# Order of the first loads of a two-layer SiLU kernel: everything on SyncE's queue, and one dummy matmul more

## The chip, the cores and the metric

One core of one Trainium2 chip. The metric is the device time of one execution in microseconds (us), taken several times; a separate execution is profiled. Kernels of one comparison ran on the same chip, alternating with the kernel before.

## The reference, cut to what matters

```python
B, S, D, F = 1, 2048, 640, 1728          # all bfloat16
h = silu(einsum("bsd,df->bsf", x, w1))
out = einsum("bsf,fd->bsd", h, w2)
```

The first product sums over D, five slabs of 128 (k = 0 to 4), for 2048 rows in four chunks of 512; the second sums over F.

## The kernel before: the parts that the change touches

TensorE needs x with D on the partitions. For chunk 0, the first slab is loaded as it lies (`xk`) and transposed on TensorE; slabs 1 to 4 come through DMA transposes. Dummy matmuls on a zero tile keep TensorE busy until `xk` has landed. `ahead_of_start` puts an instruction ahead of the program's start barrier.

```python
ld_xk = ahead_of_start(lambda: load(sp, xk[:, :, :], x_v[:, 0:SCH // P, 0:P]), ET.SP)
# ...
ld_a[0] = ahead_of_start(lambda: half(act, 0, 0), ET.Activation)   # slab 0 of w1, columns of tiles 0..3
ld_k[0] = half(act, 0, 1)                                          # slab 0, tiles 4..7
ld_a[1] = half(act, 1, 0)                                          # slab 1, tiles 0..3
ahead_of_start(lambda: first(0), ET.SP)                            # DMA transpose, k = 1 and 2
ld_k[1] = ahead_of_start(lambda: half(sp, 1, 1), ET.SP)
ahead_of_start(lambda: slab(2), ET.SP)
first(1)                                                           # DMA transpose, k = 3 and 4
slab(3)
slab(4)
# ...
wait(pe, p_z)
dummies(9)                             # ps <- z: 128x128 by 128x256
wait(pe, ld_xk, p_ident)
# ...
for h in range(2):                     # two transposes on TensorE, one copy on VectorE, twice
    # ...
# ...
wait(pe, ld_a[0], turned0[0])
k_pass(0, range(FH), 0, HB)            # four matmuls of 256 columns
wait(pe, turned0[1])
k_pass(0, range(FH), HB, SCH)          # four of 256
wait(pe, ld_k[0])
k_pass(0, range(FH, FA))               # four of 512
wait(pe, ld_x[1], ld_a[1])
k_pass(1, range(FH))
wait(pe, ld_k[1])
k_pass(1, range(FH, FA))
barrier_wait_here(ET.PE)
for k in range(2, DT):
    wait(pe, ld_x[k], ld_k[k])
    k_pass(k, range(FA))               # eight of 512
```

## Time and profile before

| | before |
|---|---|
| first three executions | 126.7, 126.93, 127.58 us |
| span of the profiled execution | 125.8 us |
| TensorE busy | 122.8 us of it, 591 matmuls |
| first real matmul starts | 3.88 us |
| matmul rate doubles at about | 9.15 us |

The first row is time on the device; all else is one execution of the profile, with times from its first instruction.

### The profile page before, as it was taken

The numbers are of one execution on the slowest core, as the hardware profiler recorded it, in microseconds if no ns is written. First come the engines' busy times: TensorE is split into PE (matmuls) and PEld (weight loads), VectorE is DVE, ScalarE is ACT, GpSimd is POOL, SyncE is SP. The second block draws the span as 40 slices with busy tenths as digits, with TensorE's granted clock in tenths as the row PEclk, the third lists the DMA queues.
The fourth block names the chain that finished last, engine by engine and source line by source line (L and its number), as shares of the span: only waits on it lengthen the run. The fifth ranks groups of instructions, "written<-read, shape, count | busy, mean of one in ns | idle before, by whom it ended". The sixth has DMA issues, their size and how long they took to land.

```text
span 125.8 us, 1358 instructions
## 1 busy us (share of the span) xinstructions
PE 122.8 (98%) x591; PEld 56.0 (45%) x591; DVE 8.0 (6%) x14; ACT 38.1 (30%) x66; POOL 0.8 (1%) x7
## 2 busy tenths in 40 slices
PE   7999999999999999999999999999999999999994
PEld 4534444444444444444444444444444443444452
DVE  0100000000000000000001020200003211012021
ACT  0400695555555555555550101010003011010100
POOL 2000000000000000000000000000000000000000
DMA  5999789895000000000000000000002767111113
GB/s 154 316 296 260 161 156 127 195 388 219 0 0 0 0 5 0 3 0 0 0 0 0 5 0 0 0 0 0 0 0 47 83 225 286 52 52 52 52 52 104
DMA packets 19557, 10.35 MB, mean 82 GB/s; under 512 B 13536, under 2 KB 19168, under 8 KB 19552
## 3 DMA queue, kind: packets, MB, share of 16 engines
q1 hardware_dynamic: 19120, 9.88, 30.1%
q10 hardware_dynamic: 432, 0.39, 0.9%
q8 instruction: 4, 0.07, 0.2%
q14 instruction: 1, 0.01, 0.0%
HBM read 4.64 MB, written 2.62 MB: 58 GB/s over the span
## 4 chain that ended last, share of the span: by engine, by line
PE 96%; DMA 2%; DVE 0%; ACT 0%; issue 0%
PE ps L218 95%; DMA xk<-in_x_dram 2%; PE ps L193 0%; DVE xT L195 0%; ACT o_sb L293 0%
## 5 line engine op out<-in xcount | busy, mean ns | idle before, releaser
L218 PE MATMUL ps<-xT,w1s 128*128 128x512 bf16 (+2 forms) x284 | 61.1, 388 | 0.3 <-DVE xT L195 0.3
L218 PE MATMUL ps<-w2s,hT 128*128 128x512 bf16 (+2 forms) x221 | 45.4, 367 | 0.0
L218 PEld LDWEIGHTS ps<-xT,w1s 128*128 128x128 bf16 (+1 forms) x284 | 27.7, 102 | 33.5 <-issue 2.7
L222 ACT ACTIVATE hT<-ps 128x512 bf16<-128x512 f32 x52 | 30.0, 608 | 28.5 <-PE ps L218 28.5
L218 PEld LDWEIGHTS ps<-w2s,hT 128*128 128x128 bf16 x221 | 20.9, 98 | 24.4 <-issue 1.1
L293 ACT CAST o_sb<-ps 128x512 bf16<-128x512 f32 (+1 forms) x8 | 4.4, 545 | 42.2 <-PE ps L218 42.2
L291 DVE CAST o_sb<-ps 128x512 bf16<-128x512 f32 (+1 forms) x9 | 6.1, 677 | 98.8 <-PE ps L218 98.8
L218 PE MATMUL ps<-hT,w2s 128*128 128x512 bf16 x52 | 11.4, 379 | 0.0
L218 PEld LDWEIGHTS ps<-hT,w2s 128*128 128x128 bf16 x52 | 5.1, 98 | 6.1
L293 ACT CAST oT<-ps 128x512 bf16<-128x512 f32 x2 | 1.1, 588 | 11.0 <-PE ps L218 11.0
L146 PE MATMUL ps<-z 128*128 128x256 bf16 x9 | 2.1, 418 | 0.4 <-DVE z L140 0.4
L203 ACT ACT_TABLE_LOAD x1 | 1.3, 1283 | 3.3 <-ACTq L409 3.3
L218 PE MATMUL ps<-w2t,hTt 64*128 64x512 bf16 (+2 forms) x17 | 2.2, 366 | 0.0
L291 DVE CAST oT<-ps 128x512 bf16<-128x512 f32 x2 | 1.3, 686 | 13.7 <-PE ps L218 13.7
L146 PEld LDWEIGHTS ps<-z 128*128 128x128 bf16 x9 | 1.2, 142 | 0.8 <-DVE z L140 0.4
L222 ACT ACTIVATE hTt<-ps 128x512 bf16<-128x512 f32 x2 | 1.2, 597 | 1.1 <-PE ps L218 1.1
L218 PEld LDWEIGHTS ps<-w2t,hTt 64*128 64x128 bf16 x17 | 0.7, 94 | 1.4 <-issue 0.8
L193 PE MATMUL ps<-ident,xk 128*128 128x128 bf16 x4 | 0.6, 308 | 0.5 <-DMA xk<-in_x_dram 0.5
L193 PEld LDWEIGHTS ps<-ident,xk 128*128 128x128 bf16 x4 | 0.3, 130 | 1.0 <-DMA xk<-in_x_dram 1.0
L195 DVE COPY xT<-ps 128x256 bf16<-128x256 bf16 x2 | 0.5, 290 | 3.1 <-PE ps L193 3.1
L218 PE MATMUL ps<-hTt,w2t 64*128 64x512 bf16 x4 | 0.6, 381 | 0.0
L218 PEld LDWEIGHTS ps<-hTt,w2t 64*128 64x128 bf16 x4 | 0.1, 94 | 0.4 <-issue 0.4
(9 smaller groups left out, 1.4 us busy)
## 6 DMA issues: line engine op xcount, KB each, us to landing
out_dram<-o_sb SPq DMA_DIRECT2D x15, 160.0 KB, 1.9
w2s<-in_w_dram SPq DMA_DIRECT2D x1, 1120.0 KB, 6.0
w2s<-in_w_dram SPq DMA_DIRECT2D x1, 960.0 KB, 8.2
w1s<-in_w_dram SPq DMA_DIRECT2D x3, 256.0 KB, 4.4
w1s<-in_w_dram SPq DMA_DIRECT2D x1, 480.0 KB, 5.2
w1s<-in_w_dram SPq DMA_DIRECT2D x1, 400.0 KB, 6.0
w1s<-in_w_dram ACTq DMA_DIRECT2D x3, 128.0 KB, 2.6
xT<-in_x_dram SPq DMA_TRANSPOSE x11, 4.2
```

Source lines behind the costliest of these rows:

```text
L146: pe.matmul(ps[:, 3, 0:HB], lhsT=z[:, 0:P], rhs=z[:, :], start=True, stop=True)
L193: ins = pe.transpose(v[:, i * P:(i + 1) * P], xk[:, 2 * h + i, :], ident[:, :])
L195: r = tick(dve.tensor_copy(out=xT[:, 0, h * HB:(h + 1) * HB], in_=v[:, 0:HB]), s_dve)
L203: act.activation(out=warm[:, :], in_=warm[:, :], func=ACT.Silu)
L218: return pe.matmul(o, lhsT=l, rhs=r, start=start, stop=stop, skip_group_check=shared)
L222: r = tick(act.activation(out=out_ap, in_=in_ap, func=ACT.Silu), s_act)
L291: r = tick(dve.tensor_copy(out=out_ap, in_=in_ap), s_dve)
L293: r = tick(act.copy(out=out_ap, in_=in_ap), s_act)
```

## The change

Its intent is visible in the diff: let nothing travel beside `xk`, bring the first slab of w1 right behind it, and fill the gap between TensorE's transposes and its first real matmul.

```diff
-        ld_a[0] = ahead_of_start(lambda: half(act, 0, 0), ET.Activation)
-        ld_k[0] = half(act, 0, 1)
-        ld_a[1] = half(act, 1, 0)
+        ld_a[0] = ahead_of_start(lambda: half(sp, 0, 0), ET.SP)
+        ld_k[0] = ahead_of_start(lambda: half(sp, 0, 1), ET.SP)
         ahead_of_start(lambda: first(0), ET.SP)
-        ld_k[1] = ahead_of_start(lambda: half(sp, 1, 1), ET.SP)
+        ahead_of_start(lambda: slab(1), ET.SP)
         ahead_of_start(lambda: slab(2), ET.SP)
@@
             turned0.append(r)
+        dummies(1)
         barrier_wait_here(ET.DVE)
@@
-        wait(pe, ld_x[1], ld_a[1])
-        k_pass(1, range(FH))
-        wait(pe, ld_k[1])
-        k_pass(1, range(FH, FA))
-        barrier_wait_here(ET.PE)
-        for k in range(2, DT):
+        for k in range(1, DT):
             wait(pe, ld_x[k], ld_k[k])
             k_pass(k, range(FA))
+            if k == 1:
+                barrier_wait_here(ET.PE)
```

## The prediction

> **What bounds the kernel now.** I read the page's chain first, then the chain in order of time, because a change to the first loads can only act ahead of the first real matmul or in gaps of TensorE.
>
> ```profile
> ## 4 chain that ended last, share of the span: by engine, by line
> PE 96%; DMA 2%; DVE 0%; ACT 0%; issue 0%
> ...
> 0.00 2.96 DMA xk<-in_x_dram
> 2.96 0.05 issue
> 3.01 0.41 PE ps L193 x2
> 3.42 0.02 issue
> 3.44 0.30 DVE xT L195
> 3.74 0.14 issue
> 3.88 120.07 PE ps L218 x577
> 123.95 0.02 issue
> 123.97 0.27 ACT o_sb L293
> ```
>
> TensorE is the bound: from 3.88 us to 123.95 us 577 matmuls follow each other and the chain names no wait. So loads after the first tile of x (xk) are hidden today. Ahead of it stand 2.96 us of waiting for xk, then 0.92 us from the first transpose to the first matmul. Only two quantities are open to this change: when that first matmul starts, and how fast the matmuls run at first.
>
> For the second I compared matmul forms in the window 0 to 14 us with those of a later window (9.4 to 9.7 us).
>
> ```profile
> L218 PE MATMUL ps<-xT,w1s 128*128 128x512 bf16 x32 | 8.8, 445 | 0.0
> L146 PE MATMUL ps<-z 128*128 128x256 bf16 x9 | 2.1, 418 | 0.4 <-DVE z L140 0.4
> L218 PE MATMUL ps<-xT,w1s 128*128 128x256 bf16 x8 | 1.9, 415 | 0.3 <-DVE xT L195 0.3
> ...
> L218 PE MATMUL ps<-xT,w1s 128*128 128x512 bf16 x3 | 0.8, 380 | 0.0
> ```
>
> Narrow windows give 634 ns for each 512-column matmul up to about 8.8 us, 540 and 414 between 9 and 9.4 us, and 379 to 380 after that. In the timeline of the weight loads the starts 8.10, 8.52, 8.95 lie 0.43 us apart; then 24 starts fall in 5.13 us, 0.214 us apart. So the rate doubles at about **9.15 us**. From 3.88 to 9.15 us TensorE ran at half rate, which costs (9.15 - 3.88) / 2 = 2.6 us. This is the larger prize. The granted clock column says 1.00 throughout, so it does not show this; spacing and duration do.
>
> Then the DMA queues, in the timeline and in narrow windows (q1 is SyncE's, q10 ScalarE's; q1 is packets, MB, share).
>
> ```profile
> 0.00 0.45 SPq L89 DMA_DIRECT2D xk<-in_x_dram  x1
> 0.12 1.47 ACTq L89 DMA_DIRECT2D w1s<-in_w_dram  x3
> ...
> 0.51 1.33 SPq L122 DMA_TRANSPOSE xT<-in_x_dram  x1
> 1.89 1.04 SPq L89 DMA_DIRECT2D w1s<-in_w_dram  x2
> 3.18 1.23 SPq L122 DMA_TRANSPOSE xT<-in_x_dram  x1
> 4.45 2.10 SPq L89 DMA_DIRECT2D w1s<-in_w_dram  x4
> ...
> q1 hardware_dynamic: 534, 0.13, 38.8%
> q10 hardware_dynamic: 199, 0.19, 36.5%
> ```
>
> The last two lines are the window 1.1 to 2.6 us. xk is 128 x 4 runs of 256 B, 512 packets, so nearly all of q1's 534 are xk. In the same time ScalarE's queue moved 0.19 MB: the halves of the first slab share the engines with xk, though the second half is needed only after 5.5 us.
>
> **What the Trainium skill says.** "DMA: Bandwidth & Descriptors", Issuing engines are not separate DMA queues: all queues run on the same 16 engines, and a second issuer saves only issue time. Queues, rings and completion order, on the same page: each engine alternates between queues packet by packet. The trace agrees: 38.8% and 36.5% side by side. With packets of 256 B against 1 KB, xk gets the smaller part of the bytes.
> "TensorE: Matmul & The Clock Gate", Part 1: the array runs at half rate until a window of about 3.4 us was busy, and the windows run freely, so the flip moves between runs. The doubling at 9.15 us agrees: two windows back is 2.3 us, and the window from 2.3 to 5.7 us holds both of TensorE's gaps. Part 4 says that a transpose does not count as busy in the same way; nothing in this trace tells.
>
> **The change, part by part.**
> 1. *The two halves of slab 0 leave ScalarE for SyncE, behind xk.* Inside xk's data time (1.1 to 2.6 us) the other queue moved 0.19 MB. Windows without xk run at 280 to 390 GB/s, so about 0.5 us of engine time is taken from xk at most; part of the trickle before 1.7 us (5 packets of q1 from 1.4 to 1.5 us) is probably latency and stays. I choose 0.4 us: xk lands at about **2.55 us** instead of 2.96. The dummies are no hindrance: the last starts at 2.08 us and occupies the array for 0.21.
> 2. *Is the first half there in time?* From ScalarE it was issued at 0.12 and landed after 2.6 us, at 2.7. Now it is issued at 0.51 behind xk; 128 KB at 350 GB/s is 0.37 us more data, landing at about 2.95 us. It is needed at 2.55 + 0.92 = 3.47 us. Hidden, with 0.5 us spare. The second half, about 3.4 us, is needed 8 x 0.213 = 1.7 us after that. Hidden.
> 3. *Two more issues ahead of the DMA transpose.* Each plain issue costs SyncE about 0.5 us (0.45, and 1.04 for two). The transpose moves from 0.51 to about 1.5 us and, with its 4.3 us to landing, from 4.8 to about 5.6 us (I grant it 0.2 for a quieter start). Slab 1, now whole and 256 KB, is issued at 2.9 us; like slab 2 today (3.2 us) it lands at about 6.1 us. Today all of k = 1 is in by 5.1 us. It is needed after the k = 0 pass, 8 x 0.213 + 4 x 0.427 = 3.4 us at half rate: 6.9 us. Hidden if TensorE stays slow; if it is fast from 4 us on, the pass ends at 5.4 and about 0.6 us shows.
> 4. *Everything later on SyncE slides by about 1 us.* Slab 3 from 4.45 + 4.4 = 8.9 to 9.8 us, slab 4 to about 10.3 us. Today k = 3 starts at about 11.7 us. Hidden. The barrier moves with SyncE by 0.5 us; ScalarE's table load then ends near 5.2 us, long before its first output at 13.75 us.
> 5. *One dummy behind the transposes.* 0.21 us in the 0.44 us between the last transpose's start (3.01 + 4 x 0.107 = 3.44) and the first matmul (3.88). It costs nothing, as the matmul still waits for VectorE's copy, and closes half of that gap. The other gap, from 2.3 us to xk's arrival, shrinks from 0.7 to 0.3 us by part 1.
> 6. *The clock.* Half-rate time after the first matmul is worth half of itself. Today no window could qualify before about 3 us, so the flip falls between roughly 6.7 and 10.3 us; this alone makes 1.8 us of spread, and the three times spread by 0.88. With the gaps smaller, windows from about 2.5 us on may qualify: start and flip come earlier together, and the flip by some 0.4 to 0.8 us more, worth 0.2 to 0.4 us. If even a window from 0.4 us qualifies, the flip comes between 3.8 and 7.2 us, worth 1 us and more.
>
> Sum: -0.4 (start) and about -0.4 (flip, my mean of the cases) on 126.93: **126.1 us**. After 15 us both kernels do the same work.
>
> **Rivals.**
> *A: nothing arrives earlier.* xk's packets trickle until 1.7 us though the engines are nearly idle, so latency or descriptor making may set its end. Then the start stays at 3.9 us, only the dummy acts, and the time is 126.6 to 127. For it: engine share of 5% in that window; against it: q10's 0.19 MB. About 30%.
> *B: start earlier, same half-rate stretch:* 126.3 to 126.5. About 35%.
> *C: the clock flips much earlier* because TensorE is busy almost without a gap from 0.39 us: 124.9 to 125.7, limited by slab 1 at 6.1 us and slab 3 at 9.8 us, which become the next waits. For it: the dummy can have no other purpose. Against it: two gaps of 0.2 to 0.3 us remain. About 30%.
> *D: a new wait replaces the old:* the first half lands later than 3.5 us, or slab 1 after 6.9 us; 127 to 128. The spare of 0.5 us speaks against it. About 5%.
>
> **Range and chances.** A to C span 124.9 to 127, and the free-running window alone moves a median of three runs by some 0.3 us. I take 125.0 to 127.1. Faster by 2% means under 124.4 us: start and flip would both have to come out at their best, 2.5 us in sum; 5%. Slower by 2% means over 129.4 us, a stall of 2.5 us in a load with 0.5 us or more spare; 2%. Within 2%: 93%.
>
> **What would show it.** xk's time to landing (3.0 us now; 2.5 to 2.6 if part 1 holds); the first matmul on w1s in the chain (3.88 now; near 3.45); the time of the change from 634 to 379 ns, against 9.15 us; a wait of TensorE for w1s or xT in the chain after it (none expected: parts 2 to 4); ScalarE's first output at 13.75 us earlier by the whole gain. The prediction is wrong if xk lands at 2.9 us or later with q10 empty, if the chain shows a DMA wait for w1s, or if the flip comes later than today by more than the start gains.

## The result, and the profile after

The changed kernel took **125.72 us** (median of 6, 125.39 to 126.03), the kernel before 127.47 us (median of 6, 126.7 to 128.23). The ratio is 0.987, 95% interval 0.983 to 0.991: faster by 1.3%, within the 2% band. A ratio here is the mean time of one kernel's fast runs over that of the other's fast runs of the same rounds, so not quite the ratio of the two medians. A second series (`r_after` below) gave 0.993, interval 0.989 to 0.997. Over all series the kernel before took 126.93 us on average (39 executions, 125.89 to 128.23) and the changed kernel 125.74 us (12 executions, 125.39 to 126.03): **1.2 us less, and a much narrower spread.** One of those 39 executions carries the mark "slow" (127.87 us); as there is one core, this mark only says that it lay over 1.5% above the fastest of its series.

The chain of the changed kernel, in order of time (start, length, what; pieces under 0.1 us ahead of the last one left out):

```profile
0.38 2.10 PE ps L146 x9
2.49 0.46 PE ps L192 x4
2.94 0.21 PE ps L146
3.21 119.01 PE ps L218 x577
122.24 0.27 ACT o_sb L290
```

The load of xk is gone from this chain, and its view of the changed kernel (`--tile xk --engine SP`) says:

```profile
DMA to landing us min/median/max: 2.3/2.3/2.3
```

It was 3.0 before. TensorE goes from dummies to transposes to one dummy to the first real matmul at **3.21 us**, 0.67 us earlier than before. That the chain no longer names xk does not mean that it stopped setting the start: xk landed at 2.29 us and the first transpose started at 2.34, and in all fourteen profiles, the one of before too, the first transpose starts 0.05 us after xk has landed. In the profile the dummies merely last a little longer (to 2.49 us) than they occupy the array. The 577 matmuls behind it now take 119.01 us where they took 120.07, though they are the same instructions: 1.06 us come from their rate. The two add up to 1.73 us, and the spans differ by 125.8 - 124.1 = 1.7. ScalarE's first output came at 12.02 us instead of 13.75, 1.73 us earlier: the whole gain is made ahead of it, as predicted.

The forms of the changed kernel's matmuls in the window 0 to 14 us:

```profile
L218 PE MATMUL ps<-xT,w1s 128*128 128x512 bf16 x40 | 9.5, 400 | 0.0
L218 PE MATMUL ps<-xT,w1s 128*128 128x256 bf16 x8 | 1.9, 415 | 0.0
```

The mean of a 512-column matmul fell from 445 to 400 ns, because fewer of them ran slow: in narrow windows they take 634 ns until 6.0 us and 380 ns from 6.6 us on. The rate doubles at about **6.35 us**, against 9.15. Slow time after the first real matmul went from 5.27 to 3.14 us; half of the difference is 1.07 us, which is the 1.06 seen in the chain.

Why xk came earlier shows in the DMA engines between 1.3 and 1.7 us. First the kernel before, then the changed one (q1 is SyncE's queue, q10 ScalarE's; packets, MB, share of 16 engines):

```profile
q1 hardware_dynamic: 56, 0.01, 14.9%
q10 hardware_dynamic: 6, 0.01, 5.9%
```

```profile
q1 hardware_dynamic: 342, 0.09, 95.4%
```

In these 0.4 us the changed kernel moved 342 packets, nearly all of xk, and the kernel before 56. The engines of the kernel before were not busy with something else: their shares add up to 21%.

Behind the start, the changed kernel's loads land later, as meant: slab 1 was issued at 2.89 us and landed after 3.3 us, at 6.2; slab 3 at 9.5. In this execution TensorE waited for none of them.

### The profile page after: what moved, and what is told of

Read it like the earlier page. It is cut to its first block, busy times and chain, and to the rows that moved or that the text cites. A ratio compares the mean times of both kernels' runs of the same rounds, so it can differ in the third digit from the quotient of the medians.

```text
span 124.1 us, 1359 instructions
## 1 busy us (share of the span) xinstructions
PE 121.8 (98%) x592; PEld 55.9 (45%) x592; DVE 8.0 (6%) x14; ACT 38.1 (31%) x66; POOL 0.8 (1%) x7
## 4 chain that ended last, share of the span: by engine, by line
PE 98%; ACT 0%; issue 0%; DVEq 0%
PE ps L218 96%; PE ps L146 2%; PE ps L192 0%; ACT o_sb L290 0%; DVEq L406 0%
## 5 line engine op out<-in xcount | busy, mean ns | idle before, releaser
L218 PE MATMUL ps<-xT,w1s 128*128 128x512 bf16 (+2 forms) x284 | 60.0, 383 | 0.0
```

The costliest lines, as they stand in the source:

```text
L218: return pe.matmul(o, lhsT=l, rhs=r, start=start, stop=stop, skip_group_check=shared)
```

## The experiments

In what follows "the doubling" is the time at which the rate of matmuls doubles, read from their lengths (about 420 to 273 ns for 256 columns, 634 to 379 ns for 512), good to some 0.2 us. A profile is a single execution; times are of six. The diffs of `e3_bystander` and `e8_tiny` leave out the spare tile and the wait for these loads at the end. The theory to be tested: (a) xk is early because ScalarE's queue is empty; (b) the doubling is a matter of its own, delayed by idle TensorE ahead of the first real matmul. Rivals: the DMA transpose behind xk was what slowed it; the doubling simply follows the first real matmul; the dummy does it all.

### What slowed xk: two loads beside it

`e3_bystander`: the changed kernel, and ScalarE loads 2 x 128 KB that nobody reads.

```diff
+        by = [ahead_of_start(lambda: load(act, spare[:, 0, :], w1_v[:, 0, 0:SCH]), ET.Activation)]
+        by.append(load(act, spare[:, 1, :], w1_v[:, 0, SCH:2 * SCH]))
         ld_a[0] = ahead_of_start(lambda: half(sp, 0, 0), ET.SP)
```

> The changed kernel, and beside it ScalarE again issues two loads of 128 KB at the places where the kernel before had its first two, into a spare tile that nobody reads. Theory (ScalarE's loads take xk's share of the engines): xk lands at 2.8 to 3.0 us instead of 2.3, the first matmul starts at 3.7 to 3.9 us or later, and 0.5 to 1.5 us of the gain is lost. Rival (the DMA transpose issued right behind xk made it slow, not ScalarE): xk still lands at 2.3 to 2.4 us, and the time stays within 0.3 us of the changed kernel.

Measured: 126.86 us (126.5 to 127.27), ratio to the kernel before 1.0005 (0.996 to 1.005): the whole gain is lost. xk landed at 3.0 us and the first real matmul started at 3.88 us, exactly as in the kernel before. Its queues from 1.3 to 1.7 us:

```profile
q1 hardware_dynamic: 34, 0.01, 8.9%
q10 hardware_dynamic: 4, 0.00, 6.3%
```

The same drought is back, though the order on SyncE is that of the changed kernel. In addition slab 1 landed so late (issued at 3.15 us, 5.0 us to landing) that TensorE waited 1.0 us for it. So the time of this run is not the price of the late xk alone: in the profile the doubling came at 7.0 us, 2.1 us earlier than in the one of before, and this wait took back what that gave. For (a) the landing counts, and not the time. The landing of xk, here and in the next run:

```profile
DMA to landing us min/median/max: 3.0/3.0/3.0
DMA to landing us min/median/max: 2.3/2.3/2.3
```

`e4_early_turn`: the changed kernel with the DMA transpose back directly behind xk; ScalarE's queue stays empty.

```diff
+        ahead_of_start(lambda: first(0), ET.SP)
         ld_a[0] = ahead_of_start(lambda: half(sp, 0, 0), ET.SP)
         ld_k[0] = ahead_of_start(lambda: half(sp, 0, 1), ET.SP)
-        ahead_of_start(lambda: first(0), ET.SP)
```

> The changed kernel with the first DMA transpose moved back to directly behind xk, ahead of the two halves of slab 0; nothing on ScalarE. Theory (ScalarE's loads were what slowed xk): xk lands at 2.3 us as in the changed kernel, but the first half of slab 0 is issued 1.3 us later and lands at about 4.5 to 5 us, so the first matmul waits for it, with a gap of over 1 us behind the dummy; time 126.7 to 128. Rival (the transpose was what slowed xk): xk lands at 2.8 us or later.

Measured: xk landed at 2.3 us, so the transpose was not what slowed it. The price is the expected one and larger: the first half of slab 0 was issued at 1.88 us and took 4.1 us to land. TensorE's timeline of this run (start, length, ..., count, idle before):

```profile
2.76 0.42 PE L146 MATMUL ps<-z 128*128 128x256 bf16 x1
6.05 10.27 PE L218 MATMUL ps<-xT,w1s 128*128 128x256 bf16 x38 [2.87 <-DMA w1s<-in_w_dram]
```

The median is 128.02 us, ratio 1.009 (1.003 to 1.015). The profiled execution (129.29 us) is marked slow; I use it for the landing of xk and of slab 0, and as one row of the table below.

`e8_tiny`: as `e3_bystander`, but 64 B per partition instead of 1 KB.

```diff
+        by = [ahead_of_start(lambda: load(act, spare[:, 0, 0:32], w1_v[:, 0, 0:32]), ET.Activation)]
+        by.append(load(act, spare[:, 1, 0:32], w1_v[:, 0, SCH:SCH + 32]))
```

> The changed kernel and two loads of ScalarE at the places of the former halves, but of only 64 B per partition (8 KB each instead of 128 KB) into a spare tile. If xk is slowed by the bytes that the other queue moves, it lands at 2.3 to 2.4 us and the time equals the changed kernel's. If it is slowed by the second queue being served at all (descriptors made, queues alternated), it lands at 2.7 to 3.0 us, as beside the loads of 128 KB.

Measured: xk at 2.4 us; 125.87 us (125.68 to 126.29), beside 125.79 for the changed kernel on the same chip. Between 1.3 and 1.7 us, xk moved 261 packets while ScalarE's queue moved 98 small ones. So a second queue as such did no harm here; loads of 1 KB per partition did. Together before, `e3_bystander`, `e4_early_turn` and the changed kernel form a square: xk lands at 3.0 us with ScalarE's 128 KB loads and at 2.3 us without, wherever the transpose stands.

### What moves the doubling

`e1_no_dummy`: the changed kernel without its added dummy.

```diff
-        dummies(1)
         barrier_wait_here(ET.DVE)
```

> The changed kernel without its one dummy behind the transposes. Theory (start and doubling of the rate are separate, and the dummy fills a gap that delays the doubling): xk still lands at 2.3 us and the first matmul on w1s still starts at 3.2 us, but the rate doubles later than the 6.35 us of the changed kernel, at 7 to 9 us, and the time is 0.3 to 1 us longer than the changed kernel's 125.7 us. Rival (the doubling comes a fixed time after the first real matmul or by chance of the window, the dummy does nothing): time within 0.2 us of the changed kernel's.

Measured: 125.96 us (125.7 to 126.2), ratio to the kernel before 0.993 (0.989 to 0.998). Its mean, 125.95 us, is 0.2 us above the changed kernel's 125.74, in the direction of the theory, but not from the same series and so not shown. The expected late doubling was a miss: it fell at about 4.7 us in the profiled execution, earlier than in the first profile of the changed kernel. TensorE's timeline of this run:

```profile
3.20 2.70 PE L217 MATMUL ps<-xT,w1s 128*128 128x256 bf16 x12 [0.26 <-DMA w1s<-in_w_dram]
7.05 4.26 PE L217 MATMUL ps<-xT,w1s 128*128 128x512 bf16 x19 [1.14 <-DMA w1s<-in_w_dram]
```

The twelve matmuls of k = 0 are done early, and then TensorE waits 1.14 us for slab 1. An early doubling does not reach the end of the kernel. This is the first sight of a floor.

`e2_dummy_only`: the kernel before plus the dummy.

```diff
             turned0.append(r)
+        dummies(1)
         barrier_wait_here(ET.DVE)
```

> The kernel before with the one dummy behind the transposes and nothing else. Theory: the first matmul stays at 3.9 us; the large gap ahead of the transposes (2.3 to 3.0 us) stays, so the doubling comes at best 0.5 us earlier: 0 to 0.4 us gained. Rival (the dummy is what counts): the doubling falls 3 us after the first matmul as in the changed kernel, at about 7 us, and about 1 us is gained.

Measured: 126.43 us (126.04 to 127.48), ratio 0.999 (0.993 to 1.004). Alone, the dummy shows no effect; in the profile the doubling was at 9.3 us, as in the kernel before.

`e5_bridge`: the kernel before, with its loads, but twelve dummies, so that TensorE has no gap while it waits for xk, and the one dummy behind.

```diff
-        dummies(9)
+        dummies(12)
@@
+        dummies(1)
         barrier_wait_here(ET.DVE)
```

> The kernel before with twelve dummies instead of nine (they then end at 2.95 us, where xk lands) and the one dummy behind the transposes; the loads as before. Theory (TensorE's gaps ahead of the first matmul delay the doubling, whatever closes them): the first matmul stays at 3.9 us, the doubling falls at 6 to 8 us, about 1 us is gained on the kernel before, with the same start. Rival (the doubling counts from the first matmul on w1s alone): no gain, 0 to 0.2 us.

Measured: ratio 0.992 (0.986 to 0.997), median 126.0 us, single executions from 125.31 to 127.45. In the profile xk landed at 3.2 us, the first real matmul started at 4.08 us, later than in the kernel before, and the doubling came at about 5.1 us: span 124.0 us. So TensorE's gaps alone, with the loads untouched and a later start, are worth 0.8% on average (interval 0.3 to 1.4%). The profiled execution is the fastest of the six. The matmuls of 512 columns between 5.7 and 6.2 us, before and in this run:

```profile
L218 PE MATMUL ps<-xT,w1s 128*128 128x512 bf16 x2 | 1.1, 634 | 0.0
L219 PE MATMUL ps<-xT,w1s 128*128 128x512 bf16 x4 | 1.0, 379 | 0.0
```

The rival that the doubling follows the first real matmul falls. The wide spread shows that closing the gaps makes an early doubling possible, not certain.

`e6_few_dummies`: the changed kernel with three dummies instead of nine at the start; TensorE idles 1.1 us ahead of its transposes.

```diff
-        dummies(9)
+        dummies(3)
```

> The changed kernel with three dummies at the start instead of nine: TensorE then idles from about 1 us to 2.3 us. The loads are those of the changed kernel. Theory (gaps delay the doubling): the first matmul stays at 3.2 us, the doubling comes later than with nine, 0.3 to 0.8 us are lost against the changed kernel. Rival (only the start of the first matmul counts): the same time as the changed kernel within 0.2 us.

Measured: 126.34 us (126.0 to 126.55); doubling at 8.2 us in the profile. `e7_two_behind`, on the same chip, differs from it in the dummies alone, with nine ahead and two behind:

```diff
-        dummies(1)
+        dummies(2)
```

> The changed kernel with two dummies behind the transposes instead of one; the second would end at 3.2 us, just where the first matmul starts. Theory: the last gap closes, start unchanged or at most 0.05 us later, the doubling no later; time equal to the changed kernel's or up to 0.3 us less. If the doubling then falls before 5 us, the wait for slab 1 (landing at 6.2 to 6.9 us) takes back what it gives.

Measured: 125.91 us (125.61 to 126.01), doubling at about 3.8 us in the profile; the mean is 0.45 us below that of `e6_few_dummies`, and only the fastest execution of `e6_few_dummies` (126.0 us) reaches the slowest of `e7_two_behind` (126.01). Some 0.1 us of it is the start (3.33 against 3.24 us); the rest is the doubling. The second dummy brings nothing that can be seen against the changed kernel (125.74 us in other series), and the profile suggests why: after the early doubling TensorE waits 1.54 us for slab 1.

All profiles; the gap is TensorE's idle time between the last dummy ahead and the first transpose, the last column the time from the first real matmul to the doubling:

| profile | gap ahead of the transposes | first real matmul | doubling | after the first matmul |
|---|---|---|---|---|
| before | 0.7 us | 3.88 | 9.15 | 5.3 |
| `e2_dummy_only` | 0.8 | 3.97 | 9.3 | 5.4 |
| `e6_few_dummies` | 1.3 | 3.33 | 8.2 | 4.9 |
| `e4_early_turn` | 0.1, then 2.9 behind | 6.05 | 11.2 | 5.2 |
| `e3_bystander` | 0.7 | 3.88 | 7.0 | 3.1 |
| changed, first profile | 0.1 | 3.21 | 6.35 | 3.1 |
| `e8_tiny` | 0.1 | 3.30 | 6.0 | 2.7 |
| `e9_slab1_act` (below) | 0.1 | 3.29 | 5.5 | 2.2 |
| `e9b_slab1_act` (below) | 0.1 | 3.25 | 5.2 | 2.0 |
| `e10_slab1_first` (below) | 0.1 | 3.27 | 4.8 | 1.5 |
| `e5_bridge` | 0.3 | 4.08 | 5.1 | 1.0 |
| `e1_no_dummy` | 0.1 | 3.20 | 4.7 | 1.5 |
| `e7_two_behind` | 0.1 | 3.24 | 3.8 | 0.6 |
| changed, second profile | 0.2 | 3.30 | 3.6 | 0.3 |

(A gap is counted from the start of the last dummy plus its 0.21 us of spacing; the idle times that the profile prints are about 0.2 us shorter, as it lets a matmul last until its result is out.) With a gap of 0.7 us or more the doubling comes 3.1 to 5.4 us after the first real matmul in these profiles; with a gap of 0.3 us or less, 0.3 to 3.1 us. Within each group it moves from one execution to the next. A row is one execution, and often an extreme one: the fastest of its six in `e5_bridge`, both `e9` runs and the first profile of the changed kernel, the slowest in `e2_dummy_only`, `e3_bystander`, `e4_early_turn`, `e10_slab1_first` and the second profile. The comparison of kernels rests on the times of six, not on this table.

Five traces (`e3_bystander`, `e5_bridge`, `e8_tiny`, `e9_slab1_act`, `e9b_slab1_act`) also hold clock records that no view prints by time. In them the full clock starts at 7.00, 5.19, 6.13, 5.53 and 5.31 us, within 0.13 us of the readings above, and lasts 119.47 us in each, which is 35 times 3.413 us, the length of window that the prediction counts with, though the spans differ by up to 2.2 us. This lets the table be sorted by an estimate, made after the fact from starts and spacings: going back from each doubling in steps of 3.41 us, the step that ends at the doubling holds at most 0.6 us of idle TensorE in every profile. The step before it lies inside the program in the first five rows, and holds 0.96 to 1.6 us there; in the others it begins ahead of the first instruction. So closing the gap matters where it brings the idle time of a step under this mark, which lies somewhere from 0.6 to 0.96 us; where the steps fall changes from one execution to the next.

### The floor, and two ways to lower it

`r_after`: the changed kernel again.

> The changed kernel again, as the measure for the other three of this call on the same chip. Expected 125.4 to 126.1 us in every run, a spread of less than half of that of the kernel before, because an early doubling is stopped by slab 1 (landing at 6.2 to 6.9 us).

Measured: 125.79 us, all six between 125.57 and 125.87, while the kernel before on this chip ranged from 125.89 to 127.87. In the profile the doubling came at 3.6 us, almost at once. TensorE's timeline of this run, and the line of its waits:

```profile
2.43 0.61 PE L192 MATMUL ps<-ident,xk 128*128 128x128 bf16 x4
2.83 0.42 PE L146 MATMUL ps<-z 128*128 128x256 bf16 x1
3.30 2.03 PE L218 MATMUL ps<-xT,w1s 128*128 128x256 bf16 x12
6.90 4.48 PE L218 MATMUL ps<-xT,w1s 128*128 128x512 bf16 x20 [1.56 <-DMA w1s<-in_w_dram]
```

```profile
PE ps L218 <- DMA w1s<-in_w_dram: 1.6, 1, 1.6
```

The first pass ends at 5.33 us, and TensorE waits until slab 1 is there; k = 1 starts at 6.90 us. The span is 124.5 us, *longer* than the 124.1 us of the first profile, where the doubling came 2.7 us later but slab 1 happened to land at 6.2 us. This would explain the narrow spread: a late doubling costs, an early one is cut off by slab 1. `e9b_slab1_act` below puts it to the test.

`e10_slab1_first`: slab 1 issued ahead of the DMA transpose.

```diff
-        ahead_of_start(lambda: first(0), ET.SP)
         ahead_of_start(lambda: slab(1), ET.SP)
+        ahead_of_start(lambda: first(0), ET.SP)
```

> The changed kernel with slab 1 issued ahead of the first DMA transpose instead of behind it; all still on SyncE. Theory (slab 1 behind the 1.3 us issue of the transpose is the floor of the changed kernel's fast runs): xk at 2.3 us, first matmul at 3.2 us, slab 1 issued at 1.5 us and landing at about 4.8 us, the transpose issued at 2.0 us and landing at 5.6 to 6 us; TensorE waits for k = 1 until 6 us at most, and the time is 0.2 to 0.6 us less than the changed kernel's on the same chip, with single runs below 125.2 us. Rival (the transpose lands as late as slab 1 did, or the doubling is rarely early enough): no gain.

Measured, on the chip of `r_after`: 125.5 us (124.95 to 125.88), mean 125.46 against 125.75, so 0.3 us less than the changed kernel; one execution was the first below 125 us. The wait for slab 1 is gone (issued at 1.5 us, landed after 3.2 us, at 4.7; the transpose after 3.7 us, at 5.7). With the doubling at 4.8 us, the profile, which is of the slowest of the six executions, shows the next floor. Its chain:

```profile
5.47 4.77 DMA w1s<-in_w_dram
10.24 0.14 issue
10.37 112.34 PE ps L218 x549
```

Slab 3, issued at 5.47 us, lands at 10.24, and TensorE waited 0.95 us for it.

`e9_slab1_act`: slab 1 in two halves from ScalarE's queue, issued only after xk has landed.

```diff
-        ahead_of_start(lambda: slab(1), ET.SP)
+        wait(act, ld_xk)
+        ld_h10 = half(act, 1, 0)
+        ld_k[1] = half(act, 1, 1)
```

(and a separate wait of TensorE for each half, as in the kernel before).

> The changed kernel with slab 1 loaded in two halves from ScalarE's queue, which first waits for xk to have landed, so that it cannot take anything from xk. Theory (once the doubling comes early, slab 1 is the next wait): xk lands at 2.3 us, the first matmul starts at 3.2 us or up to 0.2 us later, slab 1 lands at 5 to 5.6 us instead of 6.2 to 6.9, no wait for it stays; time 0 to 0.5 us less than the changed kernel's. Rival (it now takes engine time from the second half of slab 0 and the transposes, which become the wait): no gain.

Measured: 125.8 us (125.07 to 126.33), ratio to the kernel before 0.992 (0.987 to 0.996). xk at 2.4 us, doubling at 5.5 us, no wait of TensorE for a load: span 123.7 us, the shortest profile so far. Once more, beside the changed kernel (`e9b_slab1_act`, same kernel):

> Slab 1 in halves from ScalarE's queue behind a wait for xk, once more, beside the changed kernel on the same chip. Theory: no wait for slab 1 in any run, 0 to 0.5 us less than the changed kernel, with a wider spread than it (125.0 to 126.4 us), as nothing stops an early doubling. Rival: equal means, the extra queue costs at the start what it gives later.

Measured: 125.61 us (125.04 to 126.15), mean 125.61 against 125.75 for the changed kernel on the same chip, doubling at 5.2 us, span 123.7 us again. As expected the spread is wider (1.1 us, and 1.3 in the run before, against 0.3 here and 0.6 in the changed kernel's first series), as nothing cuts an early doubling off. The 0.14 us between the means is too little against this spread to be called shown. For `e10_slab1_first` the 0.3 us is about twice the uncertainty of the difference (0.13 us, from the scatter of the six and six executions); I call it likely. The two were not combined.

## Why the prediction was right, point by point

The predicted 126.1 us was 0.8 us below before's time of then; the changed kernel took 125.7 us, inside the range, and 1.2 us less than the kernel before over all series. Both mechanisms were right; both were taken too small. The number itself was a mean over cases, and the case that was given the best chance, B (126.3 to 126.5 us, 35%), did not occur: none of the 12 executions lies there. What the profiles show is C, given 30%.

1. **Part 1, xk earlier: right, but mis-sized.** 0.7 us instead of 0.4. The step that failed reads "part of the trickle before 1.7 us ... is probably latency and stays". It did not stay: 56 packets of xk became 342. I had counted the bytes that ScalarE's queue takes from xk. Some half of the loss lies in 0.4 us in which hardly anything moves on either queue: at the changed kernel's 342 packets in 0.4 us, the 286 that are missing are worth 0.33 us (an estimate). The rest fits the sharing that I had counted (from 1.7 to 2.1 us q10 took 53.6% of the engines, q1 45.0%). The 38.8% and 36.5% "side by side" were means over 1.1 to 2.6 us and hid the still part; nor did packets alternate one for one, with 162 of q1 and 73 of q10 from 1.7 to 2.1 us. Rival A, built on the same reading, falls with it.
2. **Part 2, the first half in time: right, with a smaller spare.** It landed at 0.5 + 2.6 = 3.1 us, not 2.95, and was needed at 3.2, not 3.47. The spare was 0.1 us, not 0.5; in `e6_few_dummies` TensorE even waited for it by about 0.16 us. (The wait that the profile of `e1_no_dummy` puts down to it cost nothing: the first real matmul comes 0.87 us after the first transpose there, as before and after the change.) The next gain at the start would have to move this load as well.
3. **Part 3, slab 1 hidden if TensorE is slow, showing if it is fast: right, but mis-sized.** It landed at 6.2 to 6.9 us, not 6.1, and an early doubling showed 1.1 to 1.6 us of waiting, not 0.6. The prediction contradicted itself here: it allowed for such a wait, and yet it named a DMA wait for w1s in the chain as a sign that it was wrong. The first profile has none, the second has one (DMA 3% of its chain). Nor are landing times of one profile constants: with the loads of before, all of k = 1 was in by 5.0 us in its own profile, but only by 6.6 us in `e2_dummy_only` and 6.0 in `e5_bridge`.
4. **Part 4, the rest hidden: right for the changed kernel.** Slab 3 landed at 9.5 us in the first profile (9.8 was expected). That it would be the wait after slab 1 (rival C) was seen in `e10_slab1_first`. ScalarE's table load ended at 5.6 us, not 5.2, as it moved by 1.0 us and not 0.5; it stayed hidden.
5. **Part 5, the dummy costs nothing: right.** That it helps is not shown: alone it gave 0.999, and taking it away gave 125.95 us against 125.74 in other series, too close to call. What matters is the other gap, ahead of the transposes. Rival C's argument for itself ("the dummy can have no other purpose") was a guess at an intent, not evidence.
6. **Part 6, the clock: right in kind, too small.** I weighted it with 0.4 us; the first profile shows 1.06 us, the second about 0.7 us after the wait for slab 1 (1.3 us of span less 0.6 us of start). Over all series 1.2 us less 0.6 us of start leaves 0.6 us. Both profiles of the changed kernel show case C, with the doubling 2.8 and 5.6 us earlier than in the one of before; C's time, 124.9 to 125.7 us, was met by 5 of the 12 executions; the others lie up to 0.33 us above it. That slab 1, the wait that C named, landed later than it said fits this, but is not tested by itself. The 1.8 us of spread forecast for the kernel before was about right: 1.5 to 2.0 us in its four series. Rival D did not occur.

What stays open: why xk stands nearly still from 1.3 to 1.7 us when ScalarE's loads of 1 KB per partition arrive, though the engines are then mostly idle and small loads on the same queue do not do it. `e8_tiny` made ScalarE's loads smaller and their runs shorter at once, so which of the two matters is open too. And whether the dummy behind the transposes is worth 0.2 us or nothing.

## What to carry to other kernels

In the first microseconds, give the load that everything waits for an empty machine: loads that are needed later belong behind it, also when another queue would issue them "for free" (here two of 128 KB cost 0.7 us, two of 8 KB less than 0.1). Look at the length of matmuls, not at busy time, and keep TensorE without gaps from its first dummy to its first real work; then check what the faster start runs into, since the next load in line sets the floor. When a tuned kernel's time scatters (here by 1.8%, and by 0.5% after the change), the reason for the scatter may be the thing to tune: here it gave about half of the gain.

## What the Trainium skill lacked or had wrong

- "DMA: Bandwidth & Descriptors", Issuing engines are not separate DMA queues: it says that a second issuing engine saves issue time only. It lacks that a second queue can also cost time at a kernel's start: two loads of 128 KB on ScalarE's queue moved the landing of a load of 128 KB in 256 B runs on SyncE's from 2.3 to 3.0 us, with 34 to 56 packets in 0.4 us instead of 342, and shares of the engines that add up to no more than 21%.
- Same page: for a DMA transpose it has issue times of small tiles only, none of one of this size (512 rows by 256 columns). SyncE spent 1.2 to 1.3 us on each of the first two (once 1.6, in `e3_bystander`) and mostly 0.4 to 0.6 us on a plain load. Nor does it say how long a plain load takes behind a transpose that is still in flight: the next one of 128 KB took 3.2 us to land before, and 4.1 to 4.7 in `e4_early_turn`, `e5_bridge` and `e2_dummy_only`, where 2.3 to 2.8 us was usual right behind xk.
- "TensorE: Matmul & The Clock Gate", Part 1: that the doubling waits for a busy window of about 3.4 us and moves from run to run agrees (it fell between 3.6 and 11.2 us, and the full clock lasted 35 times 3.413 us in all five traces that record it). It lacks how much idle time such a window may hold: by the estimate below the table, 0.6 us in a step did not keep the doubling away and 0.96 us did.
- Same page, Part 4: it says that a transpose does not count as busy in the same way. In the second profile of the changed kernel the rate doubled at 3.6 us although four transposes (2.43 to 3.04 us) lie in the 3.4 us before; they did not keep the doubling away. Whether they count or are only tolerated, no run tells.
- Same page, Part 1, Seeing it yourself: it warns that the recorded clock events are unreliable. It lacks that they can be missing: nine of the fourteen traces hold none, five none ahead of the doubling. The granted clock then reads 1.00 also where matmuls of 512 columns took 634 ns instead of 379.
